# Residual tiles added by DMAs behind the scaling, a third raw weight buffer, and operands made three steps ahead in a two-layer transformer block

## The chip, the cores and the metric

The kernel runs on one core of a Trainium2 chip. The metric is the device time of one execution in microseconds (us). TensorE (PE in the profile) does the matrix products, VectorE (DVE), ScalarE (ACT) and GpSimd (POOL) work on tiles, SyncE (SP) and POOL issue the DMAs.

## The reference

Attention, then a layer with a norm and a ReLU, then a Fourier mixing, then a second such layer. Batch 2, sequence 448, model width 768, hidden width 3072, all in float32:

```python
x = attention(q, k, v)                      # causal, 12 heads of 64, reshaped to (2, 448, 768)

# layer one
xn = (x - mean(x)) / sqrt(var(x) + 1e-06) * g_ln
x = x + maximum(xn @ w_ch1, 0.0) @ w_ch2

# mixing and layer two
u = x + real(fft(fft(x, axis=1), axis=2))
un = (u - mean(u)) / sqrt(var(u) + 1e-06)
out = u + maximum(un @ w_ch1_2, 0.0) @ w_ch2_2
```

## The kernel before

A tile is 128 features by 448 positions in float32. `x[b, j]` with b = 0, 1 (the batch) and j = 0 to 5 are the 12 tiles of a layer's result; `HJ` is 3. Float32 products are made of three matmuls each (`mm3`, L121 to L124: high part by high part, high by low, low by high), so every operand is split first: ACT copies the high part (L118), DVE subtracts it to get the low part (L119).

A raw weight block comes by a DMA on SP (`w_load`, L190, two buffers in `praw`), is decoded by ACT and DVE (L200, L203), combined where needed (L240, L275) and split into one of six `pw` slots. `w_tick` advances this weight work by some steps after each product; `bg_step` pops one or more entries of the list `bg`, where the other side work waits. Each engine runs its instructions in the order in which they were issued.

Each layer has three stages. The lead computes a small part plainly and gives the 12 tiles `x[b, j]` their first value. Then come the **pairs**: 10 times, `ff1_pair` makes two hidden blocks for both batches with seven products instead of eight, in the order P1, P7, P6, P2, P5, P4, P3 (`PAIR_ORDER`), each of 9 matmuls. P1, P6, P5 and P3 add up in one PSUM bank, chain `a`; between them the partial sum is read out. P6's is copied by ACT to SBUF (`kept`, L869), P5's is added by DVE, straight from PSUM, to a tile kept earlier (`added`, L873), P1's is copied by ACT into a second bank, chain `c` (L879), on which P2 goes on. P3 can only write to chain `a` when P5's value has been read, and P2 only into a `c` that has been filled. ReLU is on ACT (L722). The sums of hidden tiles that the second half needs are made by DVE (`group_sums`, L736), and all of it is spilled to DRAM by POOL (`spill`, L715).

Then come the **steps**: 35 products of 18 matmuls (18 x 0.20 us), in runs of five (P1; P5; P7 and P6 in turn; P4; P3; P2), each on a combination of weight blocks and a spilled hidden tile that SP loads back (`hr`, L267, `H_AHEAD` 2) and that ACT and DVE split (`hh`, `hl`). `w_product` (L273) makes the weights of at most `STEPS_AHEAD` = 2 products ahead. When a run ends, `done` (in `ff2_products`, L749) puts its three results into the `x` tiles: ACT copies of P1's and P5's go by accumulating DMAs on POOL (L757), P6's once by such a DMA (L775) and once by DVE (L762), P4's and P3's by DVE (L762).

The norm is applied last: all of a layer's products are made with x - mean, so the tile must be scaled by rstd = 1/std (DVE, L763, from `bg`), and the residual, parked in DRAM before the layer (`park`, L582; L575 and L577 for layer one), must not be. Before, `residual_steps` (L925) loads each of the 12 parked tiles on SP (`back`, L931), multiplies it by std (L935) and adds it to x (L936), both on DVE, in the pairs stage; the later scaling takes std out again. `invert` makes rstd by two DVE reciprocals per layer (L923) in pairs 4 and 6.

In layer one `finish` adds each ended tile into `lnsum` by a POOL DMA (`tile_sum`, L600) and, when both tiles of a column are there, puts the `fold` for the Fourier stage into `bg` (L1055; `even`, `odd` and half-folded tiles on DVE). In layer two it stores the tile to the output on SP.

Of the kernel before, what the change touches and what calls it, by code (L numbers as in the profile page):

```python
# [15 lines left out]
U16 = mybir.dt.uint16  # L16
ACTF = mybir.ActivationFunctionType
ALU = mybir.AluOpType
# [18 lines left out]
NJ = DM // P  # L37
# [7 lines left out]
SPREAD_AT = ((2, 3), (2, 3))  # L45
INVERT_AT = (3, 5)
PAIR_ORDER, PAIR_TICKS = (1, 7, 6, 2, 5, 4, 3), 2
# [18 lines left out]
GROUPS = list(range(PLAIN // 2, NCH // 2))  # L66
STEPS = [[("P1", g) for g in GROUPS], [("P5", g) for g in GROUPS], [(n, g) for g in GROUPS for n in ("P7", "P6")]]
STEPS += [[(n, g) for g in GROUPS] for n in ("P4", "P3", "P2")]
# [8 lines left out]
def fused_kernel(ctx: ExitStack, tc: tile.TileContext, aps, out):  # L77
# [9 lines left out]
    pp = ctx.enter_context(tc.tile_pool(name="pp", bufs=9))  # L87
    pd = ctx.enter_context(tc.tile_pool(name="pd", bufs=B * NJ, space=bass.MemoryType.DRAM))
# [79 lines left out]
    for moe in range(2):  # L168
        plan += [("w", moe, 1, m) for m in range(LEAD)]
        plan += [("w", moe, 2, 2 * c + u) for u in range(2) for c in range(PLAIN)]  # L170
        plan += [("pair", moe, c) for c in range(PLAIN, NCH)]
        plan += [("step", moe, name, g) for run in STEPS for name, g in run]
    for kind, moe, *at in plan:
# [12 lines left out]
    def w_load():  # L186
        if n_raw[0] < len(raw_list):
            moe, which, i = raw_list[n_raw[0]]
            t = praw.tile([P, 4 * COLS + 2], U16, tag="r", name="wraw")
            nc.sync.dma_start(out=t[:, 1 : 4 * COLS + 1], in_=aps[f"w{which}_{moe}"][i].bitcast(U16))  # L190
            w_raw.append(t)
            n_raw[0] += 1
# [68 lines left out]
    blocks, spilled, h_raw, h_list = {}, {}, {}, deque()  # L261
    steps_ready = [0]

    def h_load():
        moe, name, g = h_list.popleft()
        t = h_raw[moe, name, g] = t_tile([P, NM, S], "hr", F32)
        nc.sync.dma_start(out=t, in_=spilled.pop((moe, name, g)))  # L267

# [4 lines left out]
    def w_product(key):  # L273
        _, moe, name, g = key
        of = lambda out, a, b: nc.vector.tensor_tensor(out=out, in0=a, in1=b, op=ALU.subtract)  # L275
        while steps_ready[0] >= STEPS_AHEAD:
            yield False
# [321 lines left out]

    def tile_sum(b, j):  # L600
        if b not in ln_acc:
            ln_acc[b] = p_tile("lnsum")
            nc.gpsimd.dma_start(out=ln_acc[b], in_=x[b, j])
        else:
            nc.gpsimd.dma_start(out=ln_acc[b], in_=x[b, j], accum_op=ALU.add)

    std, rstd, xcs = {}, {}, {}
# [141 lines left out]
    def ff2_products(moe, finish, at=lambda name, g: None):  # L749
        chain, kept = {}, {}  # L750
        r1, r2 = ROWS

# [12 lines left out]
        def done(name, j, o):  # L765
            if name == "P1":
                aside(o, (r1, j))
            elif name == "P5":
                aside(o, (r1, HJ + j), (r2, HJ + j))
            elif name == "P7":  # L770
                kept[j] = aside(o)
            elif name == "P6":
                u3 = kept.pop(j)
                nc.vector.tensor_tensor(out=u3, in0=u3, in1=o, op=ALU.add)
                nc.gpsimd.dma_start(out=x[r2, j], in_=u3, accum_op=ALU.add)  # L775
                ended(r2, HJ + j, u3)
            elif name == "P4":
                ended(r2, j, o)
            elif name == "P3":
                ended(r1, HJ + j, o)  # L780
# [30 lines left out]

        for run in STEPS:
            by_tile = BY_TILE if run[0][0] == "P2" and moe == 0 else 0
# [33 lines left out]
    def pair_steps(moe, c):  # L847
# [39 lines left out]
        def p5():  # L887
            added("p7", product("P5", "a", False), 1, m + 1)

# [31 lines left out]
    def invert(b):  # L921
        rstd[b] = p_tile("rstd")
        nc.vector.reciprocal(out=rstd[b], in_=std[b])  # L923

    def residual_steps():  # L925
# [11 lines left out]

        at = [(b, j) for j in range(NJ) for b in range(B)]
        steps = [lambda a=a: fetch(*a) for a in at[:2]]
# [49 lines left out]
    def ff_middle(moe, squares, sums):  # L989
        layer[0] = moe  # L990
        h_list.extend((moe, name, g) for run in STEPS for name, g in run if g != GROUPS[-1])
        if moe == 1:
# [21 lines left out]
        for c in range(PLAIN, NCH):  # L1014
            n = c - PLAIN
            if n % 2:
                bg.extend(residuals[3 * (n // 2) : 3 * (n // 2) + 3])
            elif n:
                bg.extend(group_sums(c // 2 - 1))
            if n in INVERT_AT:  # L1020
                invert(INVERT_AT.index(n))
            ff1_pair(moe, c)
# [32 lines left out]
    def fold(b, j):  # L1055
        even, odd, f = p_tile("even", FW), p_tile("odd"), p_tile("fold", FW)
        ff = f.rearrange("p (a n) -> p a n", a=2)
        of = lambda out, op: nc.vector.tensor_tensor(out=out, in0=x[b, j], in1=x[b, HJ + j], op=op)

        def parts():  # L1060
            t = t_tile([P, 2, FW], "eo")
            split(t[:, 0], t[:, 1], even)
            eo[b, j] = t

        def middle():
# [9 lines left out]
            lambda: of(even[:, :S], ALU.add),  # L1075
            lambda: of(odd, ALU.subtract),
            lambda: (fold_rows(ff[:, 0], even, ALU.add), fold_rows(ff[:, 1], odd, ALU.subtract)),
            lambda: fold_again(even, ff),
            parts,
# [126 lines left out]
    while i < n + L_V or max([*later, *pe_later], default=0) >= i:  # L1206
# [55 lines left out]
        i += 1  # L1262
    raw_ahead[0] = 2
    while bg:
        bg_step()
    for moe in range(2):
# [12 lines left out]
        if moe == 0:  # L1279
            def finish(b, j):  # L1280
                tile_sum(b, j)
                ready.add((b, j))
                if (b, (j + HJ) % NJ) in ready:
                    bg.extend(fold(b, j % HJ))

            def loads(name, g):
                if (name, g) == ("P3", GROUPS[0]):
                    for nm in ("cd", "sd"):
# [123 lines left out]
```

## Time and profile before

| | |
|---|---|
| median of three runs | 799.65 us (798.53, 799.65, 804.9) |
| the profiled execution | 798.01 us, of which the span from first to last instruction is 796.3 us |
| PE busy | 762.9 us, 96% of the span, granted clock 0.998 |
| DVE busy | 674.4 us, 85% |
| ACT busy | 516.4 us, 65% |
| POOL busy | 122.1 us, 15% |
| stages (us from the start of the span) | attention to 97; layer one: lead to 159, pairs 159.1 to 296.7, steps 296.7 to 430.5; Fourier stage to 459; layer two: lead to 518, pairs 518.1 to 659.2, steps 659.2 to 792.6 |

In a line of a timeline the number in brackets is the time for which the engine stood idle before this instruction, with the work whose end released it. A wait of PE is time that nothing gives back; a wait of another engine matters if PE or a buffer waits for that engine next. A matmul's busy time is modelled and longer than the distance from one start to the next.

### The profile page before, as it was taken

The page shows a single profiled execution, that of the slowest core. Times are in us where ns is not written, and L with a number is a line of the kernel's source. Part 1 is how long each engine was busy: PE and PEld are TensorE (multiplying, and loading weights), DVE is VectorE, ACT ScalarE, POOL GpSimd, SP SyncE. Part 2 cuts the span into 40 slices and gives each one's busy share as a digit, 9 for nine tenths or more (in the row PEclk, how much of TensorE's full clock was granted, in tenths as well). Part 3 has the DMA queues.
Part 4 walks back from the last instruction along what each step waited for, and adds up shares of the span by engine and source line. Part 5 has one row for each costly group of instructions (what it writes and reads, how often), then busy time and mean ns, then how long its engine had stood idle before and what let it go on. Part 6 is the DMA issues. An engine that isn't in the chain of part 4 may idle for free. (4 is left out here: it accounts for less than half of the span.)

```text
span 796.3 us, 11949 instructions
## 1 busy us (share of the span) xinstructions
PE 762.9 (96%) x4263; PEld 676.0 (85%) x4263; DVE 674.4 (85%) x1101; ACT 516.4 (65%) x909; POOL 122.1 (15%) x208
## 2 busy tenths in 40 slices
PE   9999999999989999999999999989999989999898
PEld 5777789988978889989889998978988879898797
DVE  6888899969989759889999989868999739889990
ACT  7989999865746557756653467755665637757650
POOL 5654200001101101201221020001111100120100
PEclk9999999999999999999999999999999999999999
DMA  8651554357857558987966264346777547996641
GB/s 299 180 168 48 138 183 151 123 191 258 300 197 281 198 175 293 291 276 244 300 182 161 63 237 169 119 153 241 279 261 265 220 132 282 298 296 205 190 139 58
DMA packets 45003, 164.16 MB, mean 206 GB/s; under 512 B 5954, under 2 KB 16840, under 8 KB 44944
## 3 DMA queue, kind: packets, MB, share of 16 engines
q1 hardware_dynamic: 30672, 117.88, 42.8%
q0 software_dynamic: 14128, 45.29, 19.3%
q8 instruction: 33, 0.54, 0.3%
q10 hardware_dynamic: 144, 0.23, 0.1%
q14 instruction: 26, 0.21, 0.1%
HBM read 118.88 MB, written 33.95 MB: 192 GB/s over the span
## 5 line engine op out<-in xcount | busy, mean ns | idle before, releaser
L122 PE MATMUL yps<-hh,wsp 128*128 128x448 f32 x420 | 153.6, 367 | 6.8 <-DVE wsp L119 6.8
L200 ACT ACTIVATE top<-wraw 128x768 f16<-128x768 bf16 x96 | 104.7, 1091 | 80.9 <-DMA wraw<-in_w 43.3
L123 PE MATMUL yps<-hl,wsp 128*128 128x448 f32 x420 | 153.7, 366 | 1.0 <-DVE hl L119 1.0
L124 PE MATMUL yps<-hh,wsp 128*128 128x448 f32 x420 | 153.6, 366 | 0.0
L122 PE MATMUL hps<-xn,wsp 128*128 128x448 f32 x276 | 101.3, 368 | 0.0
L123 PE MATMUL hps<-xn,wsp 128*128 128x448 f32 x276 | 101.1, 366 | 0.0
L124 PE MATMUL hps<-xn,wsp 128*128 128x448 f32 x276 | 101.0, 366 | 0.0
L122 PEld LDWEIGHTS yps<-hh,wsp 128*128 128x128 f32 x420 | 78.8, 188 | 16.4 <-DVE wsp L119 9.8
L123 PEld LDWEIGHTS yps<-hl,wsp 128*128 128x128 f32 x420 | 78.9, 188 | 7.9 <-DVE hl L119 1.3
L124 PEld LDWEIGHTS yps<-hh,wsp 128*128 128x128 f32 x420 | 78.9, 188 | 6.4
L119 DVE TENSOR_TENSOR wsp<-wf,wsp 128x768 fp32r<-128x768 f32 x76 | 71.8, 953 | 13.1 <-ACT wsp L118 12.9
L715 POOL DMA_DIRECT2D hd<-r x56 | 30.2, 540 | 313.6 <-ACT r L722 250.6
L118 ACT ACTIVATE wsp<-wf 128x768 fp32r<-128x768 f32 x76 | 63.5, 842 | 20.2 <-DVE wf L240 12.1
L122 PE MATMUL hps<-xs,wsp 128*128 128x448 f32 x180 | 66.7, 371 | 9.6 <-ACT hps L879 7.5
L119 DVE TENSOR_TENSOR hl<-hr,hh 128x896 fp32r<-128x896 f32 x56 | 60.5, 1085 | 13.5 <-ACT hh L118 13.3
L118 ACT ACTIVATE wsp<-wk 128x768 fp32r<-128x768 f32 x70 | 57.5, 838 | 20.6 <-PE yps L124 12.1
L119 DVE TENSOR_TENSOR wsp<-wk,wsp 128x768 fp32r<-128x768 f32 x70 | 65.4, 951 | 1.1 <-ACT wsp L118 1.1
L124 PE MATMUL hps<-xs,wsp 128*128 128x448 f32 x180 | 66.2, 368 | 0.0
L123 PE MATMUL hps<-xs,wsp 128*128 128x448 f32 x180 | 66.0, 366 | 0.0
L203 DVE SCALAR_TENSOR_TENSOR wf<-wraw,top 128x768 uint32<-128x768 uint32 x56 | 53.4, 954 | 6.9 <-ACT top L200 5.9
L118 ACT ACTIVATE hh<-hr 128x896 fp32r<-128x896 f32 x56 | 52.3, 941 | 9.5 <-DMA hr<-hd 8.1
L122 PEld LDWEIGHTS hps<-xn,wsp 128*128 128x128 f32 x276 | 52.1, 189 | 4.4
(192 smaller groups left out, 1624.9 us busy)
## 6 DMA issues: line engine op xcount, KB each, us to landing
wraw<-in_w SPq DMA_DIRECT2D x96, 768.0 KB, 4.4
hd<-r POOLq DMA_DIRECT2D x56, 448.0 KB, 3.5
hr<-hd SPq DMA_DIRECT2D x56, 448.0 KB, 5.2
back<-xd SPq DMA_DIRECT2D x24, 224.0 KB, 4.9
x<-kept POOLq DMA_DIRECT2D x24, 224.0 KB, 7.0
qkv<-in_qk SPq DMA_DIRECT2D x11, 448.0 KB, 4.2
xd<-x POOLq DMA_DIRECT2D x18, 224.0 KB, 3.4
lnsum<-x POOLq DMA_DIRECT2D x16, 224.0 KB, 3.8
```

Of the source, the lines that this page charges most:

```text
L118: nc.scalar.activation(out=hi, in_=src, func=ACTF.Copy)
L119: nc.vector.tensor_tensor(out=lo, in0=src, in1=f32(hi), op=ALU.subtract)
L122: nc.tensor.matmul(out=dst, lhsT=w_lo, rhs=x_hi, start=first, stop=False, **kw)
L123: nc.tensor.matmul(out=dst, lhsT=w_hi, rhs=x_lo, start=False, stop=False, **kw)
L124: nc.tensor.matmul(out=dst, lhsT=w_hi, rhs=x_hi, start=False, stop=last, **kw)
L200: nc.scalar.activation(out=top_t.bitcast(F16)[:, 1::2], in_=raw.bitcast(BF16)[:, 4::4], func=ACTF.Copy)
L203: nc.vector.scalar_tensor_tensor(out=f.bitcast(U32), in0=raw.bitcast(U32)[:, 1::2], scalar=13, in1=top_t, op0=ALU.logical_shift_right, op1 ...
L715: nc.gpsimd.dma_start(out=d, in_=t)
```

## The change

- **Residuals.** Only the three tiles `x[1, 0..2]` (batch `ROWS[0]` = 1) are still loaded, multiplied by std and added in the pairs stage. For the other nine, `scale` multiplies x by rstd on DVE and then adds the parked tile by an accumulating DMA on POOL straight from DRAM; `finish` follows behind. The `scale` and `finish` of a run's three tiles are put into `bg` together, when the last of the three has its result.
- **P6's result** goes into both its targets by accumulating DMAs (six a layer instead of three DMAs and three DVE adds); four empty entries (`LANDING`) stand in `bg` ahead of its scalings.
- **Sums for the second norm.** The 12 `lnsum` DMAs go; the fold's `even` tiles (three per batch) are added up, by four DMAs.
- **Buffers.** A third raw weight buffer (three loads ahead, one in the runs that begin with P3 or P2), one tile fewer in pool `pt` (27) and in `pp` (8).
- **Steps ahead.** Weights are made three products ahead in the steps, but only one ahead while the pairs still run (`EARLY_STEPS`). In P4's run two `bg` entries go per product.
- **Reciprocals** are cut into four parts each, in `bg`.
- **P5 of a pair** is copied by ACT to SBUF (`c22`), and DVE adds from there.
- **Layer two** runs P4 and P3 mixed: P4 1, 2; P3 1; P4 3; P3 2; P4 4, 5; P3 3, 4, 5.
- The Fourier tables' first loads go one product later, and layer two's first raw loads are issued behind the last `hr` load.

```diff
-STEPS_AHEAD, H_AHEAD, STEP_TICKS, STEP_BG, BY_TILE, NEXT_EARLY = 2, 2, 5, {"P3": 4, "P2": 4}, 2, 2
+STEPS_AHEAD, H_AHEAD, STEP_TICKS, STEP_BG, BY_TILE, NEXT_EARLY, LANDING = 3, 2, 5, {"P4": 2, "P3": 4, "P2": 4}, 2, 2, 4
+AHEAD_RAW, EARLY_STEPS = (3, 1), 1
...
-    pt = ctx.enter_context(tc.tile_pool(name="pt", bufs=28))
+    pt = ctx.enter_context(tc.tile_pool(name="pt", bufs=27))
...
-    praw = ctx.enter_context(tc.tile_pool(name="praw", bufs=2))
+    praw = ctx.enter_context(tc.tile_pool(name="praw", bufs=3))
...
-        def ended(b, j, src):
+        def scale(b, j):
             t = x[b, j]
-            nc.vector.tensor_tensor(out=t, in0=t, in1=src, op=ALU.add)
-            bg.append(lambda: (nc.vector.tensor_tensor(out=t, in0=t, in1=rstd[b], op=ALU.mult), finish(b, j)))
+            nc.vector.tensor_tensor(out=t, in0=t, in1=rstd[b], op=ALU.mult)
+            nc.gpsimd.dma_start(out=t, in_=parked.pop((b, j)), accum_op=ALU.add)
+
+        def ended(*at):
+            bg.extend([lambda a=a: scale(*a) for a in at] + [lambda a=a: finish(*a) for a in at])
+
+        def added(b, j, src):
+            nc.vector.tensor_tensor(out=x[b, j], in0=x[b, j], in1=src, op=ALU.add)
...
-                nc.gpsimd.dma_start(out=x[r2, j], in_=u3, accum_op=ALU.add)
-                ended(r2, HJ + j, u3)
+                for i in (j, HJ + j):
+                    nc.gpsimd.dma_start(out=x[r2, i], in_=u3, accum_op=ALU.add)
+                if last:
+                    bg.extend([lambda: None] * LANDING)
+                    ended(*((r2, HJ + i) for i in range(HJ)))
...
         def p5():
-            added("p7", product("P5", "a", False), 1, m + 1)
+            kept("c22", product("P5", "a", False))
+            added("p7", sums.pop("c22"), 1, m + 1)
...
-        at = [(b, j) for j in range(NJ) for b in range(B)]
+        at = [(ROWS[0], j) for j in range(HJ)]
...
-            if n % 2:
-                bg.extend(residuals[3 * (n // 2) : 3 * (n // 2) + 3])
-            elif n:
+            if n == 1:
+                bg.extend(residuals)
+            elif n and n % 2 == 0:
```

How the instructions stand on ACT where layer two's pairs end: `kept<-hps` is a copy out of PSUM, `r<-...` a ReLU, `hh` and `wsp` are splits for the steps, `top<-wraw` decodes a weight block. Before:

```order
L869 ACTIVATE kept<-hps 128x448
L118 ACTIVATE wsp<-wk 128x768
L118 ACTIVATE hh<-hr 128x896
L722 ACTIVATE r<-hps 128x448 x2
L722 ACTIVATE r<-kept 128x448
L118 ACTIVATE hh<-hr 128x896
L118 ACTIVATE wsp<-wk 128x768
L722 ACTIVATE r<-kept 128x448
L879 ACTIVATE hps<-hps 128x448
```

And now:

```order
L885 ACTIVATE kept<-hps 128x448
L124 ACTIVATE wsp<-wk 128x768
L207 ACTIVATE top<-wraw 128x768
L124 ACTIVATE hh<-hr 128x896
L885 ACTIVATE kept<-hps 128x448
L722 ACTIVATE r<-hps 128x448 x2
L722 ACTIVATE r<-kept 128x448 x2
L895 ACTIVATE hps<-hps 128x448
```

One `hh` and one `wsp` of the steps have gone from between the ReLUs, and P5's copy (the second `kept`) stands ahead of them.

How the instructions stand on DVE in layer two from the last result of P6 on: `kept<-kept,yps` makes P6's result, `x<-x,rstd` is a scaling. Before:

```order
L774 TENSOR_TENSOR kept<-kept,yps 128x448
L275 TENSOR_TENSOR wk<-wk 128x768
L762 TENSOR_TENSOR x<-x,kept 128x448
L774 TENSOR_TENSOR kept<-kept,yps 128x448 x2
L762 TENSOR_TENSOR x<-x,kept 128x448 x2
L763 TENSOR_TENSOR x<-x,rstd 128x448
L119 TENSOR_TENSOR wsp<-wk,wsp 128x768
L119 TENSOR_TENSOR hl<-hr,hh 128x896
L763 TENSOR_TENSOR x<-x,rstd 128x448
```

And now:

```order
L782 TENSOR_TENSOR kept<-kept,yps 128x448
L125 TENSOR_TENSOR wsp<-wk,wsp 128x768
L782 TENSOR_TENSOR kept<-kept,yps 128x448
L125 TENSOR_TENSOR wsp<-wk,wsp 128x768
L782 TENSOR_TENSOR kept<-kept,yps 128x448
L125 TENSOR_TENSOR hl<-hr,hh 128x896
L210 SCALAR_TENSOR_TENSOR wk<-wraw,top 128x768
L763 TENSOR_TENSOR x<-x,rstd 128x448
L282 TENSOR_TENSOR wk<-wk 128x768
L125 TENSOR_TENSOR hl<-hr,hh 128x896 x2
L125 TENSOR_TENSOR wsp<-wk,wsp 128x768 x2
L763 TENSOR_TENSOR x<-x,rstd 128x448
```

The three adds of P6's result have gone, weight splits of later products stand between the results, and the first scaling waits for an accumulating DMA instead of a DVE add.

POOL issues these DMAs in layer one from the first result of P1 on (`cd`, `sd`, `cm`, `cs` and `sn` are the Fourier tables). Before:

```order
L757 DMA x<-kept 128x448 x9
L775 DMA x<-kept 128x448 x3
L603 DMA lnsum<-x 128x448
L605 DMA lnsum<-x 128x448 x2
L1031 DMA cd<-in_cd 128x772 x3
L605 DMA lnsum<-x 128x448
L1031 DMA sd<-in_sd 128x772 x3
```

And now:

```order
L758 DMA x<-kept 128x448 x9
L784 DMA x<-kept 128x448 x6
L764 DMA x<-xd 128x448 x4
L1052 DMA cd<-in_cd 128x772 x2
L764 DMA x<-xd 128x448 x2
L1052 DMA cd<-in_cd 128x772
L1052 DMA sd<-in_sd 128x772 x3
L1052 DMA cm<-in_cm 128x386
L1083 DMA even<-even 128x448
```

Two of the six additions of parked tiles stand behind loads of `cd`, which wait for free tiles of pool `pt`.

## Rows read from the trace of the kernel before

**Rows 1.** Busy time in the four stages and in 20 us of pairs; columns named first.

```profile
core 0: us, PE busy (x) PEld busy (x) DVE busy (x) ACT busy (x) POOL busy (x), PEclk, DMA share, GB/s
159.10:296.70 137.60, 130.32 (x632) 117.39 (x631) 109.32 (x152) 80.11 (x128) 15.10 (x28) 1.00 0.64 227
296.70:430.50 133.80, 130.20 (x635) 118.40 (x634) 125.72 (x168) 84.25 (x115) 23.83 (x32) 1.00 0.85 261
518.10:659.20 141.10, 132.69 (x632) 118.55 (x631) 110.86 (x155) 80.56 (x129) 15.09 (x28) 0.99 0.61 219
659.20:792.60 133.40, 129.22 (x631) 117.74 (x629) 110.38 (x130) 75.74 (x94) 10.59 (x12) 1.00 0.67 215
200.00:220.00 20.00, 20.00 (x100) 18.32 (x99) 17.54 (x28) 14.43 (x23) 2.70 (x5) 1.00 0.79 285
```

**Rows 2.** The page's costliest group: busy us, mean ns, idle before it.

```profile
L122 PE MATMUL yps<-hh,wsp 128*128 128x448 f32 x420 | 153.6, 367 | 6.8 <-DVE wsp L119 6.8
```

**Rows 3.** PE's waits in the pairs of layer one: us in total, times, longest.

```profile
PE hps L122 <- DVE kept L873: 3.4, 3, 1.6
PE hps L122 <- ACT hps L879: 2.3, 2, 1.3
PE hps L122 <- ACT kept L869: 1.5, 1, 1.5
```

**Rows 4.** PE's waits in the pairs of layer two.

```profile
PE hps L122 <- ACT hps L879: 5.3, 3, 2.9
PE hps L122 <- DVE kept L873: 2.6, 5, 0.7
PE hps L122 <- ACT kept L869: 0.5, 1, 0.5
```

**Rows 5.** PE's waits in the steps of layer one.

```profile
PE yps L122 <- DVE wsp L119: 2.6, 3, 1.1
PE yps L123 <- DVE hl L119: 1.0, 1, 1.0
```

**Rows 6.** PE's waits in the steps of layer two.

```profile
PE yps L122 <- DVE wsp L119: 4.2, 4, 1.7
```

**Rows 7.** Timeline of DVE and PE, 262 to 268 us: start, duration, instruction, idle before.

```profile
262.96 0.63 DVE L935 TENSOR_TENSOR back<-back,std 128x448 f32<-128x448 f32 x1 [2.85 <-DMA back<-xd]
...
266.38 0.61 DVE L873 TENSOR_TENSOR kept<-kept,hps 128x448 f32<-128x448 f32 x1
...
267.05 0.47 PE L122 MATMUL hps<-xs,wsh 128*128 128x448 f32 x1 [1.56 <-DVE kept L873]
```

**Rows 8.** Timeline of DVE and PE, 232 to 236 us.

```profile
232.60 0.63 DVE L935 TENSOR_TENSOR back<-back,std 128x448 f32<-128x448 f32 x1 [1.54 <-DMA back<-xd]
...
235.49 0.47 PE L122 MATMUL hps<-xs,wsp 128*128 128x448 f32 x1 [1.46 <-ACT kept L869]
```

**Rows 9.** The residual's two DVE lines: busy us, mean ns, idle before.

```profile
L935 DVE TENSOR_TENSOR back<-back,std 128x448 f32<-128x448 f32 x24 | 14.9, 621 | 8.5 <-DMA back<-xd 8.3
L936 DVE TENSOR_TENSOR x<-x,back 128x448 f32<-128x448 f32 x24 | 14.9, 621 | 0.2
```

**Rows 10.** ACT and PE at the end of layer two's pairs, and that stretch.

```profile
641.32 1.11 ACT L722 ACTIVATE r<-hps 128x448 f32<-128x448 f32 x2 [4.18 <-DMA hd<-r]
...
648.41 0.47 PE L122 MATMUL hps<-xs,wsp 128*128 128x448 f32 x1 [2.92 <-ACT hps L879]
...
649.40:652.80 3.40, 3.40 (x11) 3.04 (x10) 0.00 (x0) 0.89 (x2) 0.00 (x0) 0.50 0.30 113
```

**Rows 11.** ACT's timeline at the start of layer two's pairs.

```profile
526.99 1.09 ACT L200 ACTIVATE top<-wraw 128x768 f16<-128x768 bf16 x1 [2.50 <-DMA wraw<-in_w]
```

**Rows 12.** The accumulating DMAs of L757 (issue ns; landing), then of L775.

```profile
L757 POOL DMA_DIRECT2D x<-kept x18: 860/1214/2637, 313.6 to 698.7; - x18
DMA to landing us min/median/max: 4.3/8.7/16.9
...
DMA to landing us min/median/max: 3.1/4.8/5.5
```

**Rows 13.** DVE's timeline in the steps of layer one.

```profile
347.63 1.09 DVE L119 TENSOR_TENSOR hl<-hr,hh 128x896 fp32r<-128x896 f32 x1 [3.27 <-ACT hh L118]
```

More of the change, by code (lines that the diff above doesn't have):

```diff
@@ L171, in fused_kernel @@
         plan += [("pair", moe, c) for c in range(PLAIN, NCH)]
-        plan += [("step", moe, name, g) for run in STEPS for name, g in run]
+        plan += [("step", moe, name, g) for run in STEPS[moe] for name, g in run]
     for kind, moe, *at in plan:
@@ L189, in w_load @@
             t = praw.tile([P, 4 * COLS + 2], U16, tag="r", name="wraw")
-            nc.sync.dma_start(out=t[:, 1 : 4 * COLS + 1], in_=aps[f"w{which}_{moe}"][i].bitcast(U16))
+            with tc.issue_after(last_h[0].ins) if last_h and (moe, which, i < NM * PLAIN) == (1, 1, True) else nullcontext():
+                nc.sync.dma_start(out=t[:, 1 : 4 * COLS + 1], in_=aps[f"w{which}_{moe}"][i].bitcast(U16))
             w_raw.append(t)
@@ L266, in h_load @@
         t = h_raw[moe, name, g] = t_tile([P, NM, S], "hr", F32)
-        nc.sync.dma_start(out=t, in_=spilled.pop((moe, name, g)))
+        last_h[:] = [nc.sync.dma_start(out=t, in_=spilled.pop((moe, name, g)))]
     def h_loads():
@@ L275, in w_product @@
         of = lambda out, a, b: nc.vector.tensor_tensor(out=out, in0=a, in1=b, op=ALU.subtract)
-        while steps_ready[0] >= STEPS_AHEAD:
+        while steps_ready[0] >= steps_ahead[0]:
             yield False
@@ L598, in attention_sum @@
             nc.gpsimd.dma_start(out=ln_acc[b], in_=xa[b, pr], accum_op=ALU.add)
[L600 to L605, printed above, removed]
     std, rstd, xcs = {}, {}, {}
@@ L774, in done @@
                 nc.vector.tensor_tensor(out=u3, in0=u3, in1=o, op=ALU.add)
-                nc.gpsimd.dma_start(out=x[r2, j], in_=u3, accum_op=ALU.add)
-                ended(r2, HJ + j, u3)
+                for i in (j, HJ + j):
[3 more added lines that the diff above has]
+                    ended(*((r2, HJ + i) for i in range(HJ)))
             elif name == "P4":
-                ended(r2, j, o)
+                added(r2, j, o)
+                if last:
+                    ended(*((r2, i) for i in range(HJ)))
             elif name == "P3":
-                ended(r1, HJ + j, o)
+                added(r1, HJ + j, o)
+                if last:
+                    ended(*((r1, HJ + i) for i in range(HJ)))
             else:
@@ L810, in product @@
             bg_step(STEP_BG.get(name, 1))
-        for run in STEPS:
+        for run in STEPS[moe]:
+            raw_ahead[0] = AHEAD_RAW[run[0][0] in ("P3", "P2")]
             by_tile = BY_TILE if run[0][0] == "P2" and moe == 0 else 0
@@ L922, in invert, with part @@
         rstd[b] = p_tile("rstd")
-        nc.vector.reciprocal(out=rstd[b], in_=std[b])
+        def part(at):
+            nc.vector.reciprocal(out=rstd[b][:, at], in_=std[b][:, at])
+        return [lambda n=n: part(slice(n, n + S // INVERT_PARTS)) for n in range(0, S, S // INVERT_PARTS)]
     def residual_steps():
@@ L989, in ff_middle @@
     def ff_middle(moe, squares, sums):
-        layer[0] = moe
-        h_list.extend((moe, name, g) for run in STEPS for name, g in run if g != GROUPS[-1])
+        layer[0], raw_ahead[0], steps_ahead[0] = moe, AHEAD_RAW[0], EARLY_STEPS
+        h_list.extend((moe, name, g) for run in STEPS[moe] for name, g in run if g != GROUPS[-1])
         if moe == 1:
@@ L1055, in fold, with sums @@
     def fold(b, j):
-        even, odd, f = p_tile("even", FW), p_tile("odd"), p_tile("fold", FW)
+        even, odd, f = p_tile("even", FW), p_tile("odd", FW), p_tile("fold", FW)
         ff = f.rearrange("p (a n) -> p a n", a=2)
         of = lambda out, op: nc.vector.tensor_tensor(out=out, in0=x[b, j], in1=x[b, HJ + j], op=op)
+        def sums():
+            if b in ln_acc:
+                nc.gpsimd.dma_start(out=ln_acc[b], in_=even[:, :S], accum_op=ALU.add)
+            else:
+                ln_acc[b] = even[:, :S]
         def parts():
             t = t_tile([P, 2, FW], "eo")
-            split(t[:, 0], t[:, 1], even)
+            split(t[:, 0], t[:, 1], odd)
             eo[b, j] = t
@@ L1075, in fold @@
             lambda: of(even[:, :S], ALU.add),
-            lambda: of(odd, ALU.subtract),
-            lambda: (fold_rows(ff[:, 0], even, ALU.add), fold_rows(ff[:, 1], odd, ALU.subtract)),
-            lambda: fold_again(even, ff),
+            lambda: (of(odd[:, :S], ALU.subtract), sums()),
+            lambda: (fold_rows(ff[:, 0], even[:, :S], ALU.add), fold_rows(ff[:, 1], odd[:, :S], ALU.subtract)),
+            lambda: fold_again(odd, ff),
             parts,
```

24 lines of the change are left out of this document (15 added, 9 removed).

## The prediction

> **What bounds the kernel now.** I read the busy time by stage first. PE is busy 95 to 97% of each of the four long stages, at a granted clock of 0.99 to 1.00 [rows 1]. So the floor is the number of matmuls. In an undisturbed stretch 100 matmuls start in 20 us, 0.20 us apart [rows 1]. A stage of pairs or steps has 630 of them (10 x 7 x 9, or 35 x 18): 126.0 us. The stages took 137.6, 133.8, 141.1 and 133.4 us [rows 1], which is 11.6, 7.8, 15.1 and 7.4 us over the floor, 41.9 us together. Only this excess can be won, since the change neither adds nor removes a matmul.
>
> The waits of PE show what the excess is made of. A matmul is shown 0.367 us long [rows 2] but the next one could start 0.20 us after it; a wait shown as w therefore costs w + 0.17.
>
> - Pairs of layer one: 3.4 + 2.3 + 1.5 = 7.2 us in 7 waits [rows 3], 8.4 with the 0.17 each.
> - Pairs of layer two: 5.3 + 2.6 + 0.5 = 8.4 us in 9 waits [rows 4], 9.9 with it, and half clock behind the longest.
> - Steps: 2.6 + 1.0 = 3.6 us in 4 waits in layer one [rows 5], 4.2 us in 4 in layer two [rows 6]; 4.3 and 4.9.
>
> That is 27.5 us of 41.9; the rest are stretches in which PE's starts lie a little over 0.20 us apart and I give none of it to the change. In the steps the releaser is DVE, which lags with the weight and hidden splits, and in layer one's steps DVE is busy 125.7 of 133.8 us [rows 1]. In the pairs DVE has slack (109.3 of 137.6 us [rows 1]) but its order holds up PE: the timeline at 262 us shows DVE standing 2.85 us for a `back` load and the add that PE needs (L873) ending so late that PE stands 1.56 us [rows 7]. Another such stand of 1.54 us has a PE wait of 1.46 us 2.3 us later [rows 8].
>
> **The change, part by part.**
>
> *P5's copy on ACT.* P3's wait for L873 costs 3.4 us in 3 and 2.6 us in 5 waits [rows 3, 4], with 0.17 each 7.4 us. Now P3 waits for an ACT copy. ACT is busy 80 of 138 us here [rows 1]. The copy is one more ACT instruction per pair. ACT can be late too: its own copies already cost PE 1.5 and 0.5 us [rows 3, 4]. Bounds: 7.4 if it is never late, 0 if it inherits every wait. ACT has far more slack than DVE, so I take 5.0.
>
> *Residuals out of the pairs.* 9 of 12 tiles lose two DVE instructions of 0.62 us each [rows 9], 18 x 0.62 = 11.2 us of DVE per layer. DVE's stands for `back`, 8.3 us in all [rows 9], fall to those of three tiles. In the pairs DVE has slack, so the instructions themselves give nothing; what they give is order. The share of rows 7 is in the term above. Of the rest I count one wait, that of [rows 8]: 1.46 + 0.17 = 1.6. Bounds 0 and 1.6 plus the ACT wait of 2.3 - 1.3 = 1.0 [rows 3], 2.8. The reciprocals in four parts lie in the same slack of DVE; I give them nothing, and they cost nothing unless DVE's order again decides, which the copy on ACT takes away.
>
> *End of the pairs.* At the end of layer two's pairs ACT stood 4.18 us for a spill to land, with the copy that fills chain `c` queued behind, and PE stood 2.92 us; then it ran at granted clock 0.50, the lower level (1.2 GHz), for 3.4 us [rows 10], which loses half of that, 1.7 us. Layer one shows the same wait at 1.3 us [rows 3]. Together 2.9 + 1.3 + 2 x 0.17 + 1.7 = 6.2. Now one step instead of two is prepared that early: one `hr` and one split tile fewer are held in `pt` against one fewer in the pool, a gain of one tile, and one `hh` and one `wsp` leave ACT's queue between the ReLUs. The first ReLU still waits for a spill. Bounds 0 and 6.2; I take two thirds, 4.2.
>
> *Third raw buffer.* At the start of layer two's pairs ACT stood 2.50 us for a raw load [rows 11]; PE's waits for L879 there are 5.3 - 2.9 = 2.4 us and those for ACT's `kept` 0.5 us [rows 4], with 0.17 for three waits 3.4 us. A load that starts one block sooner covers 2.5 us easily. But not each of these waits need be the load's. Bounds 0 and 3.4; I take 2.0.
>
> *Three steps ahead, and P4 and P3 mixed, in layer two.* 4.9 us are to be had. DVE is busy 110 of 133 us [rows 1], so it can run ahead; what it lacked was permission. Against it: the scalings now wait for landings. Bounds 0 and 4.9; I take 3.3.
>
> *Layer one's steps.* Here the two halves pull against each other. 4.3 us are to be had from the third step ahead, and six P6 adds and `lnsum` DMAs go, but nine scalings that used to wait for a DVE result now have landings before or behind them: P6's scalings wait for six accumulating DMAs, the folds wait for the nine additions of parked tiles, and two of these are issued by POOL behind `cd` loads that wait for tiles. Such DMAs landed 4.3, 8.7 and 16.9 us after issue (least, median, most) for L757, and 3.1 to 5.5 us for L775 [rows 12]. The cover for P6's scalings is the four empty entries of `bg`, two products of P4 at two entries each, 2 x 3.6 = 7.2 us: more than the L775 rows, less than the L757 median. What waits behind a standing scaling is the split of the next product, covered while prepared products last (up to three, 10.8 us). I price three places (P6's scalings, the fold behind P4's, the last folds) at 0 to 3 us each and take 1.5: 4.5 lost. Of the 4.3 I count 1.5 won, since DVE is busy 94% of this stage and an `hr` that comes late (DVE stood 3.27 us for it [rows 13]) is not helped by permission to run ahead. Net -3.0; bounds -9.0 and +4.3.
>
> *At nothing:* the 12 `lnsum` DMAs less and four `even` DMAs more (POOL is busy 24 of 134 us where they stand [rows 1]); the later table loads, which have the whole of P2's run ahead of their use; the accumulating DMAs' traffic, as 18 loads go for 18 additions.
>
> Sum: 5.0 + 1.6 + 4.2 + 2.0 + 3.3 - 3.0 = 13.1 us. The profiled execution took 798.0 us, 1.65 us below the median of the runs: 798.0 - 13.1 = **785 us**.
>
> **The rivals.**
>
> *The landings are quick.* The additions behave like the fastest rows (3.1 us [rows 12]): then no scaling waits and the 4.5 us lost in layer one's steps are not lost: 785 - 4.5 = 780.5, say 781. For it: L775's most is 5.5 us, under the cover of 7.2. Against: six in a row share one queue, as L757's did. The Trainium skill, page "DMA: Bandwidth & Descriptors", section "Anatomy of one DMA — SWDGE (gpsimd) path", puts a DMA from POOL at some 2.0 us plus its bytes over 436 GB/s, an estimate of 2.5 us for 224 KB; the trace's 3.1 to 16.9 us lie above it throughout.
>
> *P3's wait passes from DVE to ACT.* ACT's queue is in order, and the copy may stand behind a ReLU that waits for a tile, as in [rows 10]. Then the 5.0 are not won: 790. For it: all three ACT waits of [rows 3, 4]. Against: ACT idles 40% of the pairs.
>
> *Tiles run short.* Three prepared steps hold more of 27 tiles than two of 28; then `hr` loads start only when PE frees a tile, and waits like that of the 1.0 us for `hl` [rows 5], 1.2 with 0.17, come some four times a layer: 785 + 8 x 1.2 = 795, about where it was.
>
> *Slower: the accumulating DMAs gate DVE.* If a landing takes 16.9 us [rows 12], DVE stands 16.9 - 7.2 = 9.7 us at a scaling or fold, and with one prepared product (3.6 us) left PE stands 6.1. Four places (three in layer one, P6's scalings in layer two) give 24 us: 785 + 24 = 809. It decides once each place costs 5.7 us ((807.6 - 785) / 4). For it: L757's issue on POOL took 0.86 us at the least but up to 2.64 [rows 12], with DVE almost never idle. Against: the long landings were in runs of nine, and L775's were short in the same stage. A page speaks for this rival: the Trainium skill, "SBUF — State Buffer", section "SBUF: two separate sides", says that some DVE instructions lock POOL out while it writes a DMA's descriptors; the stretched issues agree with it, and no row shows that this is their cause.
>
> **How the numbers follow.** Forecast 0.42, quick landings 0.13, the wait on ACT 0.18, short tiles 0.14, slower 0.13. The range runs from 775 (the forecast with the copy at 7.4, the end of the pairs at 6.2, the layer-two steps at 4.9, the raw buffer at 3.4 and layer one's loss halved: 785 - 2.4 - 2.0 - 1.6 - 1.4 - 2.2 = 775.4) to 799, which takes in short tiles with a little more; it leaves out the slower rival (0.13) and some 0.05 below. One per cent, 8 us, is about what a measurement of this kernel can tell from no change: faster is below 791.7, slower above 807.6. Faster: 0.38 of the forecast, 0.13, 0.12 of the wait on ACT, 0.03 of short tiles: 0.66. Slower: 0.11 of the slower rival and 0.01 of others: 0.12. The rest, 0.22, is the same.
>
> **What would show it.** In the pairs no wait of PE for a DVE add (P3 waits for ACT's copy or not at all) and these stages 6 to 8 us shorter each; a wait for L895 at their end under 1.2 us; layer two's steps at about 130 us; layer one's at 134 to 138, with DVE waiting at a scaling or a fold for `x<-kept` or `x<-xd`. I am wrong in the copy if PE's waits for ACT grow by what those for DVE lose; wrong in the landings if layer one's steps get shorter, or longer by over 9 us; wrong in the tiles if `hr` issues follow PE's ends and PE waits for `hl` in the steps.

## The result, and the profile after

The changed kernel took 779.97 us (median of four runs, 778.98 to 780.2), the kernel before 799.25 us. The ratio is 0.9741, 95% interval 0.9696 to 0.9787: 19.3 us less. The forecast was 785 us, the range 775 to 799.

The profiled execution has a span of 777.3 us against 796.3. The page's busy time, and the line of the raw decode, which stands in the page of before as follows:

```profile
L200 ACT ACTIVATE top<-wraw 128x768 f16<-128x768 bf16 x96 | 104.7, 1091 | 80.9 <-DMA wraw<-in_w 43.3
```

and in the page of after with no DMA as the releaser of its idle time (columns: busy, mean ns, idle before):

```profile
PE 757.8 (97%) x4263; PEld 676.5 (87%) x4263; DVE 653.9 (84%) x1071; ACT 529.1 (68%) x929; POOL 137.2 (18%) x224
...
L207 ACT ACTIVATE top<-wraw 128x768 f16<-128x768 bf16 x96 | 104.5, 1088 | 35.3 <-issue 14.2
```

The four stages of after, in the columns of [rows 1]:

```profile
159.32:289.44 130.12, 129.11 (x631) 117.93 (x630) 97.47 (x136) 82.41 (x134) 15.11 (x28) 1.00 0.60 214
289.44:424.40 134.96, 129.60 (x631) 117.80 (x630) 125.92 (x165) 87.45 (x117) 29.05 (x37) 1.00 0.91 272
513.00:643.64 130.64, 128.49 (x632) 118.03 (x630) 99.15 (x138) 83.20 (x135) 15.12 (x28) 1.00 0.58 211
643.64:773.40 129.76, 128.97 (x631) 117.90 (x629) 111.56 (x130) 79.26 (x98) 21.16 (x24) 1.00 0.82 246
```

Against [rows 1] the pairs lost 7.5 and 10.5 us, layer two's steps 3.6, and layer one's steps grew by 1.2: 20.4 us less together. The other stretches of the execution grew by 1.4, which leaves the 19.0 us by which the span is shorter. PE's waits in these stages (us in total, times, longest):

```profile
PE hps L128 <- ACT hps L895: 3.1, 4, 1.9
PE yps L128 <- DVE wsp L125: 2.8, 4, 1.3
PE yps L128 <- ACT hh L124: 1.7, 1, 1.7
PE yps L129 <- DVE hl L125: 1.3, 1, 1.3
```

That is 8.9 us in 10 waits, where before had 23.4 us in 23 [rows 3 to 6]. No wait for a DVE add is left (6.0 us in [rows 3, 4]), and none at the end of the pairs: of the four waits for L895, the largest is at the start of layer two's pairs, where before had one too. Two waits of the steps are new, 1.73 and 1.31 us. The splits that PE waits for there, `hh` on ACT and `hl` on DVE, stand behind a fold in the order of these engines, and the fold began late, because DVE had to wait for the addition of a parked tile to land. The timeline of after shows the fold, and the two stands of DVE that the landings cause in layer one:

```profile
372.02 0.62 DVE L763 TENSOR_TENSOR x<-x,rstd 128x448 f32<-128x448 f32 x1 [1.65 <-DMA x<-kept]
...
398.94 0.63 DVE L1079 TENSOR_TENSOR even<-x 128x448 f32<-128x448 f32 x1 [0.74 <-DMA x<-xd]
...
399.66 0.21 ACT L1060 ACTIVATE fold<-even 128x2 f32<-128x2 f32 x1 [3.25 <-DVE even L1079]
...
400.85 0.47 PE L128 MATMUL yps<-hh,wsp 128*128 128x448 f32 x1 [1.73 <-ACT hh L124]
402.63 0.47 PE L129 MATMUL yps<-hl,wsp 128*128 128x448 f32 x1 [1.31 <-DVE hl L125]
```

So the forecast's direction and size held. Whether its terms held is another question, and the runs below answer it mostly with no.

### The profile page after: what moved, and what is told of

Same layout as the page of the kernel before. It is cut to its first block, busy times and chain, and to the rows that moved or that the text cites. A ratio compares the mean times of both kernels' runs of the same rounds, so it can differ in the third digit from the quotient of the medians.

```text
span 777.3 us, 11977 instructions
## 1 busy us (share of the span) xinstructions
PE 757.8 (97%) x4263; PEld 676.5 (87%) x4263; DVE 653.9 (84%) x1071; ACT 529.1 (68%) x929; POOL 137.2 (18%) x224
## 5 line engine op out<-in xcount | busy, mean ns | idle before, releaser
L130 PE MATMUL hps<-xn,wsp 128*128 128x448 f32 x276 | 100.7, 365 | 0.0
```

Of the source, the lines that this page charges most:

```text
L130: nc.tensor.matmul(out=dst, lhsT=w_hi, rhs=x_hi, start=False, stop=last, **kw)
```

## The experiments

Runs that start from the changed kernel undo one part; runs that start from the kernel before make one part alone. Ratios are to the kernel before on the same chip; the medians of before there were 799.1, 797.4 and 799.8 us in the three groups.

| run | start | us | ratio, 95% interval | pairs 1 | steps 1 | pairs 2 | steps 2 |
|---|---|---|---|---|---|---|---|
| before | | 799.25 | 1 | 137.6 | 133.8 | 141.1 | 133.4 |
| after | | 779.97 | 0.9741 (0.9696 to 0.9787) | 130.1 | 135.0 | 130.6 | 129.8 |
| u_c22 | after | 780.58 | 0.9779 (0.9754 to 0.9805) | 131.8 | 135.9 | 132.5 | 128.8 |
| u_early2 | after | 781.46 | 0.9797 (0.9756 to 0.9838) | 130.9 | 136.7 | 133.3 | 133.6 |
| u_steps | after | 783.29 | 0.9793 (0.9755 to 0.9832) | 129.9 | 137.8 | 130.9 | 131.4 |
| u_lnsum | after | 796.54 | 0.9970 (0.9939 to 1.0001) | 130.4 | 144.8 | 132.6 | 129.4 |
| u_raw2 | after | 797.11 | 0.9984 (0.9956 to 1.0012) | 131.6 | 138.1 | 133.7 | 137.6 |
| d_c22 | before | 800.61 | 1.0013 (0.9985 to 1.0040) | 134.7 | 138.0 | 139.0 | 134.7 |
| d_res | before | 808.21 | 1.0129 (1.0087 to 1.0171) | 130.4 | 152.8 | 135.2 | 135.3 |
| d_noload | before | 801.18 | 1.0023 (0.9993 to 1.0053) | 138.2 | 133.1 | 142.6 | 130.5 |
| d_res_even | before | 791.04 | 0.9919 (0.9888 to 0.9950) | 130.0 | 138.0 | 135.7 | 131.9 |
| d_raw3 | before | 793.31 | 0.9913 (0.9880 to 0.9947) | 136.7 | 132.1 | 137.5 | 131.3 |
| i_spread | after | 780.01 | 0.9759 (0.9712 to 0.9807) | 130.0 | 136.0 | 132.2 | 130.1 |
| i_both | after | 784.90 | 0.9815 (0.9768 to 0.9863) | 129.9 | 139.1 | 132.5 | 130.4 |

The stages are of one profiled execution each; a stage whose work is the same in two runs differs by 1 to 2 us between them.

The changed kernel was not run again in these groups, so what an undone part costs can be taken from the times or from the ratios: 0.6 or 3.0 us for u_c22, 1.5 or 4.5 for u_early2, 3.3 or 4.2 for u_steps, 16.6 or 18.3 for u_lnsum, 17.1 or 19.4 for u_raw2. The text gives the times. The reciprocals in parts, the later first table loads and the raw loads behind the last `hr` load were not run alone.

### P5's copy: undone, and alone

```diff
-            kept("c22", product("P5", "a", False))
-            added("p7", sums.pop("c22"), 1, m + 1)
+            added("p7", product("P5", "a", False), 1, m + 1)
```

> The changed kernel with P5's value again added by DVE straight from PSUM, everything else as changed. Theory A (the gains of the pairs have separate sources, and the copy is worth 5 to 7.4 us of them): the two stages of pairs get longer by 5 to 7 us together, 785 to 787 us, with PE's waits for DVE's add back. Theory B (DVE was late only because the residual loads held up its order; with them gone the copy has nothing to hide): pairs as in the changed kernel within 1 us, 780 to 781 us.

The kernel before with the two lines the other way round:

> The kernel before with P5's copy to SBUF by ACT and nothing else. Theory A: PE's 8 waits for DVE's add (6.0 us, 7.4 with what the modelled ends hide) go and no wait of ACT takes their place: 799.3 - 5 to 7 = 792 to 794 us. Theory B: the add's lateness passes into later waits (the ReLU of its result, the weight splits of the next pair): at most 2 us, 797 to 799 us.

Undone, the pairs of the profiled execution are 3.5 us longer, little more than such stages differ by anyway, and the time 0.6 us (within its uncertainty): nearer to theory B. PE's waits for the add come back as two, 1.3 us together, not the 6.0 of [rows 3, 4]. Alone, the copy gains nothing in time. PE's waits in layer two's pairs of that run:

```profile
PE hps L122 <- ACT hps L879: 6.5, 5, 2.8
PE hps L122 <- ACT kept L869: 2.5, 3, 1.8
```

The 2.6 us for DVE's add are gone and those for ACT have gone from 5.8 to 9.0 [rows 4]: in layer two the rival "P3's wait passes from DVE to ACT" is what the copy does by itself. In layer one PE's waits in the pairs fall from 7.2 to 5.1 us. The pairs of this profiled execution are 5.0 us shorter together and its steps 5.5 us longer, with one wait of 3.0 us for a weight split at 328 us; whether the copy causes the longer steps is not shown.

### The residuals' part alone

The edit is the `scale`, `ended`, `added`, P6 and `residual_steps` parts of the diff above, with `LANDING` and the two entries per product in P4; `tile_sum` stays in `finish`.

> The kernel before with the residuals' part alone: three tiles still loaded in the pairs, nine added by DMAs behind the scaling, P6's result by DMAs into both targets, four empty entries, scalings ahead of finishes, two entries per product in P4; the sums of layer one, the buffers, the steps ahead, the copy and the order of layer two as before. Theory A: pairs 2 to 4 us shorter together (the waits behind the loads), steps of layer one 1 to 5 us longer (landings, and twelve sums that wait for them): 797 to 802 us. Theory B: pairs 8 us shorter or more, 792 us or less.

The pairs came out by theory B, 7.2 and 5.9 us shorter, and without a wait of PE at their end, although two steps are prepared early as before. The time came out 9 us longer than before, which neither theory had. DVE and PE in layer one's steps:

```profile
408.58 0.63 DVE L1072 TENSOR_TENSOR even<-x 128x448 f32<-128x448 f32 x1 [13.57 <-DMA x<-xd]
...
410.81 0.74 PE L123 MATMUL yps<-hl,wsp 128*128 128x448 f32 x1 [13.18 <-DVE hl L119]
```

and POOL before it (start, duration of the issue, idle before it):

```profile
384.99 0.57 POOL L603 DMA_DIRECT2D lnsum<-x  x1 [10.12 <-DMA x<-xd]
...
397.73 1.26 POOL L763 DMA_DIRECT2D x<-xd  x1
```

Each `lnsum` DMA waits for the addition of its tile to land (the first one for 10.12 us). POOL's order is one line, so the next additions wait with it, DVE's fold waits for them, and the splits of the next product stand behind the fold. The addition that the fold waits for was issued at 397.73 us and landed at 408.49. In the run with the `even` sums below, the same addition was issued at 392.17 and landed at 397.52. So about half of these 11 us is POOL's line, and the other half a slower landing, with four table loads issued just ahead of it.

### The sums: undone, and together with the residuals

`tile_sum` back in `finish`, the `even<-even` DMAs out:

> The changed kernel with layer one's sums as before: each finished tile is added to lnsum by a DMA on POOL (12 of them) instead of adding up the fold's even tiles (4). Theory D (twelve sums that each wait for an addition of a parked tile to land stand in POOL's order ahead of later additions, and the folds wait behind; the run of the residuals' part alone lost 17.4 us in two waits there): layer one's steps 10 to 17 us longer, 790 to 797 us. Theory E (with three steps ahead the waits are covered, the loss alone was that of two steps ahead): at most 3 us, 780 to 783 us.

Theory D: 16.6 us longer, nearly all that the change had won. In the steps PE stands 10.6 us for a split on ACT. That split stands behind a part of the fold, and the fold waits for an addition that was issued behind an `lnsum` DMA. In the Fourier stage PE stands again, behind the last `lnsum` DMAs, of which each waits for the one ahead of it:

```profile
383.08 0.57 POOL L610 DMA_DIRECT2D lnsum<-x  x1 [10.41 <-DMA x<-xd]
...
397.10 1.23 POOL L771 DMA_DIRECT2D x<-xd  x1
...
401.97 0.63 DVE L1086 TENSOR_TENSOR even<-x 128x448 f32<-128x448 f32 x1 [10.53 <-DMA x<-xd]
...
408.56 1.86 PE L128 MATMUL yps<-hh,wsp 128*128 128x448 f32 x4 [10.59 <-ACT hh L124]
...
452.09 0.86 POOL L612 DMA_DIRECT2D lnsum<-x  x1 [2.80 <-DMA lnsum<-x]
...
455.21 0.60 ACT L124 ACTIVATE ms<-lnsum 128x448 fp32r<-128x448 f32 x1 [9.20 <-DMA lnsum<-x]
...
457.06 0.35 PE L128 MATMUL mixps<-cs,ab 113*1 113x226 f32 x1 [3.37 <-DVE x L1155]
```

The steps of layer one are 9.8 us longer than in after, just short of the 10 that theory D gave as the least, and the stretch from there to layer two's pairs is 5.7 us longer. The stretch from the start of these steps to 440 us is

```profile
289.49:440.00 150.51, 137.70 (x664) 125.29 (x663) 133.17 (x183) 88.63 (x124) 34.77 (x44) 0.95 0.87 259
```

Three steps ahead do not cover it. The mean granted clock of the stretch falls to 0.95: it stood at 0.50, the lower level, when PE began again after its long stand. The kernel before with the residuals' part and the `even` sums:

> The kernel before with the residuals' part and the sums over the fold's even tiles, nothing else. Theory D: the pairs keep their 13 us gain of the run with the residuals' part alone, and layer one's steps come back to within 5 us of before: 787 to 792 us. Theory E: the steps stay 10 us or more too long, 800 us or more.

791 us, 0.8% less than before: theory D again. Its pairs:

```profile
160.70:290.68 129.98, 128.81 (x631) 117.60 (x630) 100.73 (x134) 80.23 (x128) 15.18 (x28) 1.00 0.63 224
516.60:652.30 135.70, 131.40 (x632) 119.07 (x631) 102.60 (x137) 81.10 (x130) 15.19 (x28) 0.99 0.59 213
```

With neither the copy nor the third buffer nor fewer early steps, 13.0 of the 18.0 us that the pairs lost in all are there.

### Loads or work

```diff
-            back[b, j] = p_tile("back")
-            nc.sync.dma_start(out=back[b, j], in_=parked.pop((b, j)))
+            parked.pop((b, j))
...
-            t = back.pop((b, j))
-            nc.vector.tensor_tensor(out=t, in0=t, in1=std[b], op=ALU.mult)
+            t = p_tile("back")
+            nc.vector.tensor_tensor(out=t, in0=x[b, j], in1=std[b], op=ALU.mult)
```

> The kernel before without the loads of the parked residual tiles: DVE does the same two operations for each of the 12 tiles, but multiplies the tile x itself by std, so the residual is left out of the result and no DVE instruction of the pairs waits for a load. Theory F (what the residuals cost the pairs is DVE's stand at the loads, 8.3 us of idle time, which is late for everything behind it): the pairs of the two layers get 10 to 13 us shorter together, 787 to 790 us. Theory G (it is the work, 24 x 2 x 0.62 us = 30 us in DVE's queue): pairs within 3 us of before, 797 to 800 us.

Theory G. The pairs are 0.6 and 1.5 us longer, not 10 shorter. The time, 801.2 us, is a little over G's range. No stand of DVE at a load is left, but PE's waits in the pairs are 16.3 us where before had 15.6. DVE now stands at group sums, 2.4 to 2.8 us four times, and each time PE waits 2.5 to 2.8 us for the add behind. One of these stands waits for a spill:

```profile
252.31 1.09 DVE L736 TENSOR_TENSOR r<-r 128x896 f32<-128x896 f32 x1 [2.69 <-DMA hd<-r]
253.32 1.82 DVE L119 TENSOR_TENSOR wsp<-wf,wsp 128x768 fp32r<-128x768 f32 x2
255.06 0.61 DVE L873 TENSOR_TENSOR kept<-kept,hps 128x448 f32<-128x448 f32 x1
...
255.73 0.47 PE L122 MATMUL hps<-xs,wsh 128*128 128x448 f32 x1 [2.84 <-DVE kept L873]
```

The kernel before already had a stand of this kind, so not even there was every such wait of PE the load's:

```profile
219.76 1.09 DVE L736 TENSOR_TENSOR r<-r 128x896 f32<-128x896 f32 x1 [2.38 <-DMA hd<-r]
...
224.65 0.48 PE L122 MATMUL hps<-xs,wsh 128*128 128x448 f32 x1 [1.58 <-DVE kept L873]
```

So taking the loads away gives nothing while the work stays; taking both away, for nine tiles of twelve, gives 13 us. With the work its entries in `bg` go too, so the time on DVE and the places in the order are not told apart, and how the work makes the group sums late was not followed instruction by instruction.

### The third raw buffer: undone, and alone

Undone: `praw` with two buffers, `AHEAD_RAW` (2, 1).

> The changed kernel with two raw weight buffers and loads two ahead (one in the runs that begin with P3 or P2). My prediction put the third buffer at 2.0 us, between 0 and 3.4, at the start of layer two's pairs: 780 to 783 us, with ACT waiting for wraw loads again. Rival: with residual loads gone from SP the raw loads are early enough with two buffers, under 0.7 us: 780.0 to 780.7 us; or it also fed the steps, where DMA share is 0.8 to 0.9: over 784 us.

17.1 us longer, the last rival. Layer two's steps alone lose 7.8 us. ACT's waits for raw loads are back (before had 43.3 us):

```profile
ACT top L207 <- DMA wraw<-in_w: 49.7, 31, 4.6
```

One of them in the timeline, from ACT to PE:

```profile
683.46 1.09 ACT L207 ACTIVATE top<-wraw 128x768 f16<-128x768 bf16 x1 [3.12 <-DMA wraw<-in_w]
...
686.46 0.95 DVE L125 TENSOR_TENSOR wsp<-wk,wsp 128x768 fp32r<-128x768 f32 x1
...
687.46 0.47 PE L128 MATMUL yps<-hh,wsp 128*128 128x448 f32 x1 [2.71 <-DVE wsp L125]
```

PE's wait is booked on DVE's weight split. That split stands behind the decode, which DVE starts when ACT's part ends (at 684.6 us), and ACT's part waited for the raw load: two engines back from PE. (The profile books DVE's start on a matmul that ended at about the same time; the link to ACT is read from the times.) Alone in the kernel before, with `raw_ahead` 3 throughout:

> The kernel before with the third raw weight buffer (three loads ahead throughout; one tile fewer in pools pt and pp to make room) and nothing else. Theory H (ACT's waits for raw loads, 43.3 us, were a bound of the steps by themselves): the two stages of steps 6 us shorter together or more, 793 us or less. Theory I (before, DVE's residual work and the permission to prepare only two steps set the pace, and the buffer pays only once these are gone): within 3 us of before.

793.3 us, 0.9% less: between the theories by time, for the steps are 1.7 and 2.1 us shorter and the pairs 0.9 and 3.6. ACT's waits for raw loads fall from 43.3 us to

```profile
ACT top L200 <- DMA wraw<-in_w: 1.3, 1, 1.3
```

so some 35 of these 42 us were not on the path in before, if the 6.9 us won all come from them. In the changed kernel more of it is. The accumulating DMAs raise the DMA share of layer two's steps from 0.67 [rows 1] to 0.82; that this is why was not tested.

### Steps: ahead, early, and mixed

Two steps ahead instead of three, and P4 and P3 one behind the other in layer two:

> The changed kernel with two steps ahead instead of three and with layer two's P4 and P3 one behind the other. Layer one's steps show the price of the third step alone, layer two's that of both. My prediction: 3.3 us of layer two's steps (0 to 4.9) and 1.5 of layer one's: 783 to 787 us. Rival (the third raw buffer alone keeps the steps fed): within 1 us of the changed kernel. Rival (the landings are covered only by the third step): over 788 us, with PE waiting for splits behind scalings.

3.3 us longer: 2.9 in layer one's steps (the third step alone) and 1.7 in layer two's (both). My terms were 1.5 and 3.3; their sum stands, their split does not. Unless the third step costs time there, mixing is worth at most 1.7 us, no more than such stages differ by.

`EARLY_STEPS` 2 instead of 1:

> The changed kernel with two steps prepared while the pairs run instead of one. Theory A (the wait at the end of the pairs, 1.3 and 2.9 us with half clock behind the longer, was one of tiles and of ACT's order, and fewer early steps ended it): the waits for the copy into chain c come back at the end of the pairs, 3 to 6 us, 783 to 786 us. Theory C (it was ended by P5's copy ahead of the waiting ReLU, or by fewer other tiles in use): no wait of PE over 0.5 us there, 779 to 781 us.

Between the two: a wait of 0.72 us comes back at the end of each layer's pairs (not 1.3 and 2.9), the time is 1.5 us longer, within its uncertainty. This profiled execution was the longest of its four runs, and its steps show what a late landing costs:

```profile
730.20 0.62 DVE L763 TENSOR_TENSOR x<-x,rstd 128x448 f32<-128x448 f32 x1 [5.82 <-DMA x<-kept]
...
734.62 0.47 PE L128 MATMUL yps<-hh,wsp 128*128 128x448 f32 x1 [3.26 <-DVE wsp L125]
```

In after, stands of 1.6 and 2.3 us at the same line cost PE nothing.

### Two attempts at a better version

P5's accumulating DMAs from `bg`, one per product:

```diff
-                nc.gpsimd.dma_start(out=x[b, j], in_=t, accum_op=ALU.add)
+                bg.append(lambda b=b, j=j: nc.gpsimd.dma_start(out=x[b, j], in_=t, accum_op=ALU.add))
```

> The changed kernel with the six accumulating DMAs of P5's results issued one per product from bg instead of at once. In the changed kernel they land 3.5 to 15.0 us after issue at 326 to 344 us, the hidden tiles loaded beside them took 8 to 10 us, and PE stood 1.3 us. If the crowd of DMAs is the cause, that wait (and 0.7 us at the same place in layer two) goes: 777.5 to 779 us. If the raw loads beside them set it, or if the additions now come late for the scalings: 780 to 782 us.

780.0 us, the time of the changed kernel. The edit did not spread the DMAs. POOL issued them at 325.25 to 328.21 us, as close together as in after (325.93 to 328.91):

```profile
325.25 5.32 POOL L758 DMA_DIRECT2D x<-kept  x6 [16.09 <-ACT kept L756]
```

POOL had nothing else to wait for, so a place later in the list did not delay them. Whether the crowd costs anything stays open. The wait at 343 us was 0.3 us here instead of 1.3, but in u_lnsum, whose six DMAs are issued as in after, no wait stands there at all: it changes from one execution to the next. With the Fourier tables five products later as well:

```diff
-                if (name, g) == ("P3", GROUPS[1]):
+                if (name, g) == ("P2", GROUPS[0]):
...
-                if (name, g) == ("P2", GROUPS[0]) and ("cs", 0) not in dft:
+                if (name, g) == ("P2", GROUPS[2]) and ("cs", 0) not in dft:
```

> The same with the Fourier tables loaded five products later as well (cd, sd, cm at the first product of P2, cs and sn at its third). In the changed kernel two additions of parked tiles land 6.4 and 8.0 us after issue behind these loads, two hidden tiles take 6.5 and 7.4 us, and PE stands 1.7 and 1.3 us. If the tables' traffic is the cause, layer one's steps lose another 3 us: 775 to 777 us. If the tables then come late for the Fourier stage, it waits there by as much or more: 778 to 782 us.

This edit did move the loads, and the two waits at 400 us went, as they should if the tables' traffic was their cause. Larger ones came, in P2 and in the Fourier stage:

```profile
417.43 0.74 PE L128 MATMUL yps<-hh,wsp 128*128 128x448 f32 x1 [3.64 <-ACT hh L124]
...
438.71 0.43 PE L128 MATMUL abps<-cd,eo 128*113 128x386 f32 x1 [2.03 <-DVE eo L125]
```

784.9 us. In the 6 us from 418 and from 440 us, behind these waits, the granted clock is 0.55 and 0.54, near the lower level of 0.50. Neither wait is for a table: the last one landed at 431.4 us, and PE waits for splits behind ACT's and DVE's other work. Why these are late is not shown. No version beat the changed kernel.

## Why the prediction was right, and which of its steps were not

**The frame held.** The time that could be won was the excess of the four stages over 126 us each, and PE's waits made up most of it. (The list counts seven waits in [rows 3], which has six, so the 27.5 us are 27.3; no term rests on it.) With the 0.17 us added to each, PE's waits in the stages fell by 16.7 us, most of the 19.3; those for DVE's add and at the end of the pairs are gone, as forecast. Every sign that the prediction named for the stages came true except one (layer two's pairs lost 10.5 us, not 6 to 8). But these signs cannot tell the terms apart, and most terms were wrong:

**Residuals out of the pairs (1.6 us, bounds 0 and 2.8): mis-sized, 13 us.** The step that failed is "in the pairs DVE has slack, so the instructions themselves give nothing". DVE was busy 109 of 137.6 us [rows 1], but its work stood in PE's way by its place in the order, and 17 us less of it over the two layers' pairs (109.3 to 100.7 and 110.9 to 102.6) took PE's waits there from 15.6 to 5.5 us (d_res_even). Gone with it are most of the wait for DVE's add (1.9 of 6.0 us are left) and the whole wait at the end of the pairs, which I had given to other terms. I had read the releaser of DVE's idle time (the load, [rows 7, 8]) as the cause; without loads the waits stayed.

**P5's copy (5.0): too large.** 0 alone, 0.6 us of time and 3.5 us of the pairs when undone. Most of the wait that it was to end was already gone with the residuals' work.

**End of the pairs (4.2): the wait went, but for another reason.** It ended with the residuals' part, with two steps prepared early as before; fewer early steps give some 0.7 us per layer on top.

**Third raw buffer (2.0, bounds 0 and 3.4): mis-sized, 6.9 us alone and 17 when undone.** I priced it at PE's waits at the start of layer two's pairs, 2.2 us of which are one wait in before:

```profile
524.08 0.47 PE L122 MATMUL hps<-xs,wsp 128*128 128x448 f32 x1 [2.17 <-ACT hps L879]
```

It ended at 524.08 us, and ACT's stand for the raw load [rows 11] began only at 524.49, so the load could not be its cause. The wait (now for L895) is still there in after:

```profile
517.18 1.06 ACT L207 ACTIVATE top<-wraw 128x768 f16<-128x768 bf16 x1 [0.90 <-ACT wsp L124]
518.12 0.56 ACT L895 ACTIVATE hps<-hps 128x448 f32<-128x448 f32 x1
...
518.73 0.47 PE L128 MATMUL hps<-xs,wsp 128*128 128x448 f32 x1 [1.95 <-ACT hps L895]
```

The copy stands behind a decode in ACT's order, and every raw load issued before 517 us had landed by then. The row that I should have priced, 43.3 us of ACT's idle time ahead of L200, was on the page and not in my sum; 25 us of it lie in the steps. Undone, 10.9 us are lost in the steps and 4.6 in the pairs; alone, the buffer gave 3.8 and 4.5. Why it is worth more in the changed kernel stays open.

**Three steps ahead and mixed (3.3 and 1.5): the sum right**, 3.3 us when undone.

**Landings in layer one's steps (4.5 lost): about right.** With the residuals' part and the `even` sums alone the stage grew by 4.2 us. The third step gives 2.9 back where I had 1.5, and the buffer, which I had not counted in this stage, has a share in it too (3.1 when undone); so the stage grew by 1.2 us where I had 3.0. In the changed kernel the scalings' stands (1.6 us here, 2.3 in layer two) were covered; the two waits behind the fold cost PE 3.0.

**"At nothing", the sums: wrong, 16.6 us.** I named POOL's 24 busy of 134 us as the cover. What counts is how long POOL's line stands. The slower rival was real: it said 809 us, and the residuals' part alone took 808.2. It named only the landings, though, where about half of the delay was POOL's line. What kept it away is the part of the change that I had priced at zero.

Parts made alone give 6.5 (residuals and sums) and 6.9 us (third buffer), by their ratios; undoing the steps, the early steps and the copy costs 3.3, 1.5 and 0.6. That adds up to 18.8 of 19.3, but with ratios throughout it would be 25, and the single uncertainties are 2 to 4 us: the agreement shows little. Undoing the buffer costs 17 us, so it is worth far more in the finished kernel than ahead of it. The sums are worth 17 in both, once the residuals' part is in (808.2 against 791.0 us ahead of it); without that part they were not run. My 13.1 was thus a sum of terms too large and too small, and that 785 lay so near to 780 was in good part luck.

## What to carry to other kernels

An engine with 20% of slack can still set the pace by what stands in its order; cost the work that is taken out of a queue by the waits behind it, and ask of every wait whether it would stay if only its named releaser were gone. Follow a releaser back more than one engine: a split that is late may be late for a load two engines earlier. When results start to arrive by DMA, every DMA that reads them becomes a wait in its queue's line; change these in the same edit. And see in the timeline that an edit moved what it was to move, before its result is read as an answer.

## What the runs showed of the hardware

- Six accumulating DMAs issued together on POOL landed one behind the other. P5's six in layer one of after, issued at 325.9 to 328.9 us, landed between 329.4 and 343.9, some 2.9 us apart; P6's six, issued at 366.0 to 368.7, between 370.8 and 380.6, some 2.0 apart. Three hidden tiles loaded on SP from 330 to 337 us, beside P5's, took 9 to 10 us where the median of all is 5.5.
- The issues of P6's six are shown longer and longer, 0.87 us for the first, some 0.35 more for each behind it, 2.64 for the sixth. So an issue can look stretched, as in [rows 12], only because others stand ahead of it.
- The landings of after's accumulations (from issue, least, median, most; P1's and P5's, then P6's, then the parked tiles'):

```profile
DMA to landing us min/median/max: 3.4/9.1/15.0
...
DMA to landing us min/median/max: 4.8/7.4/11.9
...
DMA to landing us min/median/max: 3.7/5.9/10.6
```

- A reciprocal of 128x448 took 2.94 us on DVE before; its quarters of 128x112 take 0.84 us each, 3.4 together.
